# Ranking the first expert's work ahead of the last routing in an attention and mixture-of-experts kernel

## The chip, the cores and the metric

The kernel runs on one core of one Trainium2 chip. The metric is the time of one execution on the device in microseconds (us); a kernel's time is the median of several runs. Beside the runs there is one profiled execution, with a trace of every instruction. The engines are called as in the profile: PE is TensorE (PEld its weight loads), DVE is VectorE, ACT is ScalarE, POOL is GpSimd, and SP is SyncE, which here only issues DMA transfers (SPq in the trace).

## The reference

Two stages. The first is a recurrent attention over 768 steps with a 40 x 40 state per batch entry and head (4 entries, 8 heads):

```python
for t in range(S):
    y[:, :, t] = np.einsum('bhd,bhde->bhe', rt, state)
    Sa = np.einsum('bhde,bhe->bhd', state, at)
    state_decay = state * wt[:, :, None, :] - np.einsum('bhd,bhe->bhde', Sa, bt)
    state = state_decay + np.einsum('bhd,bhe->bhde', vt, kt)
```

Its output is reshaped to 3072 tokens of width 320. The second stage is a mixture of 8 experts. Each token gets noisy logits, `x @ w_gate + log1p(exp(x @ w_noise)) * noise`, and goes to the two experts with the largest ones, with weights from a softmax over the two:

```python
h = np.maximum(x[mask] @ w1[e], 0.0)
out[mask] += top2_w[mask, k, None] * (h @ w2[e])
```

The hidden width is 1024, so w1 is 320 x 1024 and w2 is 1024 x 320 for each expert.

## The kernel before

**Stages.** The attention is computed in chunks of 64 steps. It runs in 24 steps n = 0 to 23 (`Att.run`): 12 chunks for each of two halves of the batch. Each step ends with one tile of 128 tokens (`xt`), which is stored in DRAM (`xd`) and goes to `logits`: three transposes on PE (`px`, L107), a high and a low half of the transposed tile (`xT`; L108 on ACT, L109 on DVE), nine small matmuls (`pl`, L111), and a copy of the 16 logits to `lg` (L115, ACT).

**Routing.** The 24 tiles are routed in groups of 8, 8, 4, 2 and 2 (`RTS`). When a group is complete, `route` finds the top two experts (`gate`: some twenty small DVE instructions and four on ACT), adds the logits to a check sum (`acc`, L133, POOL), counts the tokens for each expert (`cnt`, L135), ranks them with small matmuls against the counts so far (`pr`, L137 to L140), adds the counts to `cumh` (L142, POOL, one addition for each tile of the group), and computes the row `po` at which each entry goes into the experts' list. `scatter` (L162) then writes the entries to that list (`ls`) in DRAM with one indirect DMA on POOL for each tile and choice. The check sum is read only by `flag`, at the end, which decides whether a slower general path must run.

**Two lists.** The list and the token store exist twice. The first 20 tiles (`NA=20`) go to `ls[0]` and `xd[0]`; `turn` then copies the list to `ls[1]`, and the last two groups (tiles 20 and 21, 22 and 23) are scattered only there. The first 512 rows of expert 0 (`PARTS[0]`) are read from `ls[0]` and `xd[0]`, everything else from `ls[1]` and `xd[1]`.

**Experts.** `experts` loads w1 and w2 of an expert (`load1`, L207 and L208; `load2`, L212; on SP). `loadx` loads a part of the expert's index list (`le`, L240, SP) and gathers the tokens, 128 in each indirect DMA on POOL (`xr`, L241). `split1` and `split2` cut the weights into a high part (`w1h`, L218; `w2h`, L226; ACT) and a low part (L219, L220, L227; DVE). `trans` transposes the tokens on PE (`pt`, L254) and splits them (L257 to L261). `hidden` is the first layer: for each of eight blocks of 128 hidden units eight matmuls (`ph`, L273), then the positive part, split into `hh` (L274, ACT) and `hl` (L276, DVE). `output` is the second layer: for each tile of up to 128 tokens 24 matmuls (`po`, L295), a weighting (L296), and an indirect DMA that adds the rows to the output (L297, POOL). An expert has two parts, 512 and 320 rows. For expert 0 the second part is gathered after the last scatter, and its transposes stand after the first part's outputs in the program.

**Memory.** The experts' SBUF and PSUM pools are opened after those of the attention are closed and lie on the same memory. All eight PSUM banks are in use on both sides.

**Order.** The program is traced in Python, and a planner orders each engine's instructions: it simulates the engines, and whenever one is free it issues, of the instructions that its simulation has as ready, the one with the best rank. The rank is the place in the traced program. `high_priority(offset=n)` ranks a block as if it stood n instructions earlier; the chain of the attention's state has 1500 (`PRIO`), and the block of the first expert has `PX`, which is 0. `burst` keeps a group of matmuls together. `issue_after` puts instructions behind a given one on their engine. Each engine then works through its instructions strictly in that order, waiting for semaphores.

Of the kernel before, what the change touches and what calls it, by code (L numbers as in the profile page):

```python
# [13 lines left out]
ALU = mybir.AluOpType  # L14
# [7 lines left out]
NA=20  # L22
FAR=65536
XS,WS=2.0**10,2.0**4
PX=0
SG=1
MRB=1
NOUT=3072+896
# [13 lines left out]
class Moe:  # L42
# [84 lines left out]
    def route(s,n0,T,ps,tag,bufs):  # L127

        nc=s.nc
        w=s.ent[:,n0:n0+T,:,2]  # L130
        lg=s.lg[:,0:T]
        oh=s.gate(lg,s.nz[:,n0:n0+T],T,w[:,:,0],w[:,:,1])
        nc.gpsimd.tensor_tensor(s.acc[:,0:T],s.acc[:,0:T],lg,op=ALU.add)  # L133
        r=lambda name,sh=(8,),dt=F32: s.rp.tile([128,RT,*sh],dt,name=name)[:,0:T]
        cnt=r("cnt",dt=F16); nc.vector.tensor_tensor(cnt,oh[:,:,0],oh[:,:,1],op=ALU.add)  # L135
        pr=ps.tile([128,T,8],F32,name="pr",tag=tag,bufs=bufs)
        nc.tensor.matmul(pr,s.tri,cnt,start=True,stop=False,skip_group_check=True)  # L137
        nc.tensor.matmul(pr,s.ones,s.cumh.rearrange("p (o e)->p o e",o=1).to_broadcast([128,T,8]),start=False,stop=False,skip_group_check=True)
        for j in range(T-1):
            nc.tensor.matmul(pr[:,j+1:],s.ones,cnt[:,j:j+1].to_broadcast([128,T-1-j,8]),start=False,stop=j==T-2,skip_group_check=True)  # L140
        h=s.rp.tile([128,8],F16,name="cumh",bufs=len(RTS)); p=s.cumh
        for j in range(T): nc.gpsimd.tensor_tensor(h,p,cnt[:,j],op=ALU.add); p=h  # L142
        s.cumh=h
        rk=r("rk",(1,8))
        k1,k2=r("k1"),r("k2"); bc=lambda z: z.to_broadcast([128,T,8])
        nc.vector.tensor_tensor(k1,pr,bc(s.lim),op=ALU.is_gt)
        nc.vector.tensor_tensor(k2,pr,bc(s.lim2),op=ALU.is_gt)
        nc.vector.tensor_tensor(k1,k1,bc(s.jump),op=ALU.mult)
        nc.vector.scalar_tensor_tensor(k2,k2,float(FAR),pr,op0=ALU.mult,op1=ALU.add)
        nc.vector.tensor_tensor(rk[:,:,0],k1,k2,op=ALU.add)  # L150
        nc.vector.tensor_tensor(oh,oh,rk.to_broadcast([128,T,2,8]),op=ALU.mult)
        pf=r("pf",(2,)); nc.vector.tensor_reduce(pf,oh,axis=AX.X,op=ALU.add)
        po=s.po[:,n0:n0+T]
        nc.vector.scalar_tensor_tensor(po,pf,float(FAR),s.junk[:,n0:n0+T],op0=ALU.add,op1=ALU.min)
        s.todo+=range(n0,n0+T)
        if n0+T>=(NA if SG else 0):
            with (s.tc.issue_after(s.sg) if s.sg else ExitStack()): s.scatter()
# [165 lines left out]
    def experts(s,after):  # L323
        s.adds={}
        with s.tc.issue_after(after): r1=s.load1(0); r2=s.load2(0)
        with s.tc.high_priority(offset=PX):
            x=s.loadx(0); W1=s.split1(r1); X=s.trans(x[0])
        s.loadx(0,x,1); W2=s.split2(r2)
        for e in range(E_):
            if e+1<E_: r1=s.load1(e+1); xn=s.loadx(e+1); s.loadx(e+1,xn,1); r2=s.load2(e+1)  # L330
            with (s.tc.high_priority(offset=PX) if e==0 else ExitStack()): H0=s.hidden(W1,X,0)
            if e==0: s.output(W2,H0,x,e,0); s.trans(x[0],X,1)
# [549 lines left out]
```

## Time and profile before

| | |
|---|---|
| runs before, us | 1023.14, 1027.94, 1027.19 (median 1027.19) |
| profiled execution, us | 1021.33, its span 1019.5 |
| PE busy | 767.5 us, 75% of the span |
| PE weight load busy | 681.2 us, 67% |
| DVE busy | 492.1 us, 48% |
| ACT busy | 396.1 us, 39% |
| POOL busy | 521.4 us, 51% |
| mean granted PE clock | 0.936 |

The span is from the first to the last instruction of the trace. A row of an engine's order of time reads: start, duration, engine, line, operation, output and input tiles, count, and in brackets how long the engine had been idle before it and what ended that. A row of the waits reads: engine, line, what it waited for, total us, count, longest us. In the chain of waits each row is start, length and what the end of the program was waiting for at that time. The attention's last tile is transposed (L107) at 571.78 us; the last instruction of the trace ends at 1019.5 us.

### The profile page before, as it was taken

The page shows a single profiled execution, that of the slowest core. Times are in us where ns is not written, and L with a number is a line of the kernel's source. Part 1 is how long each engine was busy: PE and PEld are TensorE (multiplying, and loading weights), DVE is VectorE, ACT ScalarE, POOL GpSimd, SP SyncE. Part 2 cuts the span into 40 slices and gives each one's busy share as a digit, 9 for nine tenths or more (in the row PEclk, how much of TensorE's full clock was granted, in tenths as well). Part 3 has the DMA queues.
Part 4 walks back from the last instruction along what each step waited for, and adds up shares of the span by engine and source line. Part 5 has one row for each costly group of instructions (what it writes and reads, how often), then busy time and mean ns, then how long its engine had stood idle before and what let it go on. Part 6 is the DMA issues. An engine that isn't in the chain of part 4 may idle for free.

```text
span 1019.5 us, 25178 instructions
## 1 busy us (share of the span) xinstructions
PE 767.5 (75%) x10506; PEld 681.2 (67%) x10506; DVE 492.1 (48%) x961; ACT 396.1 (39%) x816; POOL 521.4 (51%) x678
## 2 busy tenths in 40 slices
PE   0110117687877687899799379999999999999995
PEld 0110116576666576787688259899999989999995
DVE  9329525355567556447355542643434334443430
ACT  2213213354444344554454322543434334343421
POOL 6259979237967728818874335133333333333313
PEclk9999999797778787999899779999999999999998
DMA  3799963478479557655355843426262525262303
GB/s 96 188 203 226 242 172 90 116 197 225 127 193 241 146 121 204 175 152 146 96 120 148 272 119 68 131 49 150 49 150 49 150 49 149 50 149 51 36 7 40
DMA packets 135264, 136.21 MB, mean 134 GB/s; under 512 B 67392, under 2 KB 114948, under 8 KB 135060
## 3 DMA queue, kind: packets, MB, share of 16 engines
q1 hardware_dynamic: 123492, 117.35, 43.6%
q0 software_dynamic: 11648, 17.15, 9.6%
q8 instruction: 85, 1.39, 0.6%
q14 instruction: 39, 0.32, 0.1%
HBM read 96.48 MB, written 41.37 MB: 135 GB/s over the span
## 4 chain that ended last, share of the span: by engine, by line
PE 43%; POOL 21%; DMA 14%; issue 8%; DVE 6%; SPq 3%; ACT 3%; POOLq 0%; DVEq 0%; ACTq 0%
PE po L295 16%; PE ph L273 12%; POOL Tt L541 7%; POOL X L542 7%; PE pY L441 2%; PE psc L441 2%; PE pW L441 2%; DMA X<-scr 2%; DMA xr<-xd,le 2%; DMA out_dram<-y,le 2%; DMA d_ab<-pk 2%; DMA rawk<-in_fm_dram 2%; PE pt L254 2%; POOL rawk L515 2%; POOL xr L241 1%
## 5 line engine op out<-in xcount | busy, mean ns | idle before, releaser
L297 POOL DMA_INDIRECT out_dram<-y,le x56 | 92.4, 1651 | 201.2 <-ACT y L296 171.9
L276 DVE SCALAR_TENSOR_TENSOR hl<-ph,hh 128x256 fp32r<-128x256 f32 (+1 forms) x128 | 71.0, 556 | 154.0 <-ACT hh L274 153.6
L274 ACT ACTIVATE hh<-ph 128x320 fp32r<-128x320 f32 (+1 forms) x128 | 66.1, 518 | 156.1 <-PE ph L273 155.9
L541 POOL TENSOR_TENSOR Tt<-X 128x30 f32<-128x30 f32 (+9 forms) x180 | 108.8, 604 | 11.8
L542 POOL TENSOR_TENSOR X<-X,Tt 128x30 f32<-128x30 f32 (+9 forms) x180 | 106.3, 590 | 12.6
L241 POOL DMA_INDIRECT xr<-xd,le x56 | 54.0, 965 | 74.4 <-DMA le<-ls 27.9
L441 PEld LDWEIGHTS <-st_ab 120*64 120x64 f16 (+1 forms) x928 | 26.5, 117 | 75.8 <-issue 42.2
L295 PE MATMUL po<-w2h,hh 128*128 128x320 f32 x384 | 74.6, 314 | 0.0
L441 PE MATMUL pQ<-w,dT 128*128 128x40 f16 x1152 | 41.2, 184 | 42.3 <-DMA dT<-scr 33.5
L273 PE MATMUL ph<-xh,w1h 128*128 128x512 f32 (+1 forms) x256 | 71.3, 362 | 0.5 <-ACT xh L257 0.5
L441 PEld LDWEIGHTS <-dT 128*128 128x128 f16 x1152 | 38.2, 100 | 49.6 <-DMA dT<-scr 34.4
L273 PE MATMUL ph<-xh,w1l 128*128 128x512 f32 (+1 forms) x256 | 69.0, 351 | 0.0
L273 PE MATMUL ph<-xl,w1h 128*128 128x512 f32 (+1 forms) x256 | 68.6, 349 | 0.0
L295 PE MATMUL po<-w2l,hh 128*128 128x320 f32 x384 | 68.3, 312 | 0.0
L295 PE MATMUL po<-w2h,hl 128*128 128x320 f32 x384 | 68.1, 309 | 0.0
L441 PE MATMUL psc<-st_ab 120*64 120x64 f16 x384 | 12.6, 215 | 68.1 <-DMA st_ab<-d_ab 29.6
L295 PEld LDWEIGHTS po<-w2h,hh 128*128 128x128 f32 x384 | 61.3, 188 | 3.1
L441 PE MATMUL psc<-RV,uT 128*64 128x128 f32 x384 | 56.5, 294 | 4.1 <-DVE P L665 3.7
L295 PEld LDWEIGHTS po<-w2h,hl 128*128 128x128 f32 x384 | 59.2, 188 | 0.1
L295 PEld LDWEIGHTS po<-w2l,hh 128*128 128x128 f32 x384 | 58.9, 188 | 0.4
L162 POOL DMA_INDIRECT ls<-ent,po x48 | 47.2, 984 | 19.3 <-issue 13.6
L441 PE MATMUL psc<-RV 128*64 128x128 f32 x384 | 56.6, 294 | 0.0
(285 smaller groups left out, 1893.9 us busy)
## 6 DMA issues: line engine op xcount, KB each, us to landing
w2r<-in_w_dram SPq DMA_DIRECT2D x8, 1280.0 KB
RV<-in_rv_dram SPq DMA_DIRECT2D x48, 192.0 KB
rawba<-in_fm_dram SPq DMA_DIRECT2D x24, 360.0 KB
d_ab<-pk SPq DMA_DIRECT2D x24, 360.0 KB
st_ab<-d_ab SPq DMA_DIRECT2D x36, 240.0 KB
w1r<-in_w_dram SPq DMA_DIRECT2D x8, 1024.0 KB
raww<-in_fm_dram SPq DMA_DIRECT2D x12, 365.6 KB
st_ab<-d_ab SPq DMA_DIRECT2D x24, 180.0 KB
```

The source lines that it names most:

```text
L162: st=nc.gpsimd.indirect_dma_start(out=s.ls[s.half],out_offset=OFFS(ap=po[:,j,k:k+1],axis=0),in_=s.ent[:,j,k],in_offset=None)
L241: for k in range(c,c+a): nc.gpsimd.indirect_dma_start(out=x[:p,k],out_offset=None,in_=s.xd[w],in_offset=OFFS(ap=li[:p,k,0:1],axis=0))
L254: for t,p in tiles(t0,n): nc.tensor.transpose(pt[:,t-t0:t-t0+p],x[:p,t//128,f0:f0+128],s.idm[:p,:p])
L273: for i,(a,b) in enumerate(mm): nc.tensor.matmul(ph[:,:n],a,b,start=i==0,stop=i==7)
L274: nc.scalar.activation(hh[:,f,:n],ph[:,:n],AF.Relu)
L276: if c.stop>c.start: nc.vector.scalar_tensor_tensor(o,ph[:,c],0.0,hh[:,f,c].bitcast(F32),op0=ALU.max,op1=ALU.subtract)
L295: nc.tensor.matmul(po[:p],h[:,f,r],w[:,f],start=k==0,stop=k==23); k+=1
L297: st=nc.gpsimd.indirect_dma_start(out=s.out_d,out_offset=OFFS(ap=idx[:p,ii],axis=0),in_=y[:p],in_offset=None,compute_op=ALU.add)
L441: def mm(s,*a,**k): return lambda: s.nc.tensor.matmul(*a,**k)
L515: k1=k_[:,:,:,64*b:64*b+64]; (nc.vector if g in MK else nc.gpsimd).tensor_tensor(k1,k1,G['NH'].rearrange("p (a c b) t->p b c a t",a=3,c=CG ...
L541: eng.tensor_tensor(t,Xt[:,j:j+1,j+1:].to_broadcast([128,j,m]),Xt[:,0:j,j:j+1].to_broadcast([128,j,m]),op=ALU.mult)
L542: s.tl=eng.tensor_tensor(Xt[:,0:j,j+1:],Xt[:,0:j,j+1:],t,op=ALU.add)
```

## The change

Three edits. `PX` goes from 0 to 2500. The check sum of the logits is added on DVE for each of the five groups. The counts are added on DVE for the last group alone (22 + 2 > 22; for the group before it is 20 + 2, which is not), and stay on POOL for the others.

```diff
-PX=0
+PX=2500
@@ route
-        nc.gpsimd.tensor_tensor(s.acc[:,0:T],s.acc[:,0:T],lg,op=ALU.add)
+        nc.vector.tensor_tensor(s.acc[:,0:T],s.acc[:,0:T],lg,op=ALU.add)
@@
-        for j in range(T): nc.gpsimd.tensor_tensor(h,p,cnt[:,j],op=ALU.add); p=h
+        for j in range(T): (nc.vector if n0+T>22 else nc.gpsimd).tensor_tensor(h,p,cnt[:,j],op=ALU.add); p=h
```

`PX` is used in two places of `experts`, which are unchanged. The first covers, for expert 0, the list and the gathers of part 0, the split of w1 and the transposes of part 0. The second covers the first layer of part 0. The loads of w1 and w2, the second part's list and gathers, and the split of w2 are outside both.

```python
with s.tc.issue_after(after): r1=s.load1(0); r2=s.load2(0)
with s.tc.high_priority(offset=PX):
    x=s.loadx(0); W1=s.split1(r1); X=s.trans(x[0])
s.loadx(0,x,1); W2=s.split2(r2)
for e in range(E_):
    ...
    with (s.tc.high_priority(offset=PX) if e==0 else ExitStack()): H0=s.hidden(W1,X,0)
```

## The prediction

> **What bounds the kernel now.** I read the windows around the change from attention to experts first, then each engine's order of time there, then SyncE's waits and the chain of waits. The page gives the span; the windows show where TensorE (PE) is not the bound.
>
> ```profile
> span 1019.5 us, 25178 instructions
> ```
> ```profile
> 576.00:598.00 22.00, 6.89 (x32) 4.58 (x33) 14.09 (x55) 7.88 (x15) 9.47 (x11) 0.50 0.90 287
> 598.00:620.00 22.00, 20.55 (x106) 17.09 (x105) 9.07 (x16) 7.71 (x15) 8.52 (x9) 0.98 0.21 56
> ```
>
> Columns: length, busy us and count of PE, PE weight load, DVE, ACT, POOL, then granted clock, DMA share, GB/s. From 598 on PE is busy 20.55 of 22 us at nearly full clock. Between the attention and the first expert, from 576 to 598, it works 6.89 of 22 us at half clock. Whatever brings the dense part forward is carried to the end, since nothing but PE sets the pace behind it. What filled the gap, PE and then POOL in order of time:
>
> ```profile
> 571.78 0.55 PE L107 MATMUL px<-idm,xt 128*128 128x128 f32 x3 [0.65 <-DVE xt L676]
> 578.25 0.25 PE L111 MATMUL pl<-wg,xT 128*128 128x16 f16 x3 [5.92 <-ACT xT L108]
> 579.79 0.33 PE L111 MATMUL pl<-wg,xT 128*128 128x16 f16 x6 [1.29 <-DVE xT L109]
> 587.70 0.19 PE L137 MATMUL pr<-cnt,tri 128*128 128x16 f16 x1 [7.58 <-DVE cnt L135]
> ...
> 590.26 0.21 PE L317 MATMUL pf<-okh,ones 128*128 128x5 f16 x1
> ...
> 593.02 1.21 PE L254 MATMUL pt<-idm,xr 128*128 128x128 f32 x4 [0.71 <-DMA xr<-xd,le]
> 594.71 2.93 PE L273 MATMUL ph<-xh,w1h 128*128 128x512 f32 x6 [0.47 <-ACT xh L257]
> ...
> 599.78 0.51 PE L273 MATMUL ph<-x,w1h 128*128 128x512 f32 x1 [1.29 <-ACT x L260]
> ```
> ```profile
> 580.42 0.67 POOL L133 TENSOR_TENSOR acc<-acc,lg 128x32 f32<-128x32 f32 x1 [13.73 <-ACT lg L115]
> 582.13 1.48 POOL L241 DMA_INDIRECT xr<-xd,le  x1 [1.03 <-DMA xd<-xt]
> ...
> 586.60 0.95 POOL L241 DMA_INDIRECT xr<-xd,le  x1 [0.30 <-issue]
> ```
>
> The four gathers of expert 0's first 512 rows (L241) need only tokens routed long before, yet they stand behind the check sum (L133), for which POOL sat idle 13.7 us. PE's first expert matmuls wait for those gathers; dense work starts at 599.78. The index list le that the gathers read is not early either, as SyncE's (SP) queue shows:
>
> ```profile
> 567.84 0.38 SPq L207 DMA_DIRECT2D w1r<-in_w_dram  x1
> ...
> 570.51 0.73 SPq L212 DMA_DIRECT2D w2r<-in_w_dram  x1
> 571.29 1.34 SPq L240 DMA_DIRECT2D le<-ls  x1
> ```
> ```profile
> SPq L207 <- PE pgm L442: 4.3, 1, 4.3
> ```
>
> The weight load w1r waited for the last pgm (L442, the reader of the attention's last NG_ tile), because the experts' tiles lie on the attention's memory. The same release holds le and xr, so nothing of the expert moves before 567.84. That caps the gain.
>
> **The change, step by step.** Against the profiled execution: 1021.33 us, span 1019.5 plus 1.83 around it. The median shown, 1027.19, is 5.9 above it; I subtract the same gain from the median.
>
> *Step 1, le on SP.* `loadx(0)` is now ranked 2500 instructions earlier, while the loads of w1r and w2r are outside that block. All three come free at 567.84, so I expect le first, at 567.84 in place of 571.29. The three weight issues slide by le's own issue, at most 1.34 us. A quiet le and the gathers behind it can be read from the chain of waits:
>
> ```profile
> 596.75 1.61 DMA le<-ls
> ...
> 601.71 3.03 DMA xr<-xd,le
> 604.78 0.33 PE pt L254 x2
> ```
> ```profile
> 599.17 0.97 POOL L241 DMA_INDIRECT xr<-xd,le  x1 [4.58 <-DMA le<-ls]
> ```
>
> le landed 1.61 after its issue (596.75 to 598.36), and POOL began 0.81 later. So the first gather may start at 567.84 + 1.61 + 0.81 = 570.3, provided L133 is not in front: it goes to DVE, and POOL has nothing else queued between the scatters before 567 and the last routing's counts and scatters, which the gathers pass. What waits behind a gather that waits for le is only these, and they come ready after 587. On SP le passes the weights alone; the last token store and a fill of the output slide with them and nobody near waits for those.
>
> *Step 2, four gathers on POOL.* Loaded: from the first start, 582.13, to the last transposes fed by them, 593.02, is 10.9. Quiet: three spacings of 1.27 (from 599.17 to 601.71 there are two) plus 3.03 is 6.8. The DMA share of 0.90 over 576 to 598 says loaded: 570.3 + 10.9 = 581.2. The lower end is 577.1.
>
> *Step 3, w1 splits.* In the order of ACT and DVE before:
>
> ```profile
> 575.82 2.00 ACT L218 ACTIVATE w1h<-w1r 128x1024 fp32r<-128x1024 f32 x2 [7.54 <-DMA w1r<-in_w_dram]
> 577.72 0.47 ACT L108 ACTIVATE xT<-px 128x384 f16<-128x384 f32 x1
> 578.29 1.06 ACT L218 ACTIVATE w1h<-w1r 128x1024 fp32r<-128x1024 f32 x1
> 580.15 0.18 ACT L115 ACTIVATE lg<-pl 128x16 f32<-128x16 f32 x1 [0.80 <-PE pl L111]
> 581.15 1.99 ACT L226 ACTIVATE w2h<-w2r 128x640 fp32r<-128x640 f32 x3 [0.81 <-DMA w2r<-in_w_dram]
> ```
> ```profile
> 579.76 1.22 DVE L220 TENSOR_TENSOR w1h<-w1r,w1h 64x1024 fp32r<-64x1024 f32 x1
> ...
> 581.13 0.29 DVE L305 TENSOR_TENSOR fz<-acc 128x128 f32<-128x128 f32 x1
> ...
> 594.69 1.29 DVE L258 TENSOR_TENSOR xl<-pt,xh 128x512 fp32r<-128x512 f32 x2 [3.33 <-ACT xh L257]
> 599.76 1.40 DVE L261 TENSOR_TENSOR x3l<-pt,x 64x512 fp32r<-64x512 f32 x2 [3.78 <-ACT x L260]
> ```
>
> They ended at 580.98 (579.76 + 1.22); with le's 0.4 to 1.34 in front, by 582.3. The gathers come later, so the splits are no bound.
>
> *Step 4, dense start.* From the last transposes (593.02) to dense matmuls (599.78) took 6.8: evictions, six half-clock matmuls, the third transposes. 581.2 + 6.8 = 588.0, or 583.9 with quiet gathers.
>
> *Step 5, the routing that is overtaken.* The third w1h (1.06) now stands ahead of xT, and L220 (1.22) ahead of xT's second half (L109), so pl ends about 0.5 + 1.2 later, at 581.8. From lg (580.15) to pr (587.70) took 7.5; the part-0 evictions add about 2.7 on DVE (the L258 pair 1.29, the L261 pair 1.40). pr becomes ready near 592. PE issues in order: if pr stands before the dense matmuls, they wait until 592.0; if behind, they start at 588.0. I take the middle, 590.0. Behind a waiting pr are queued all of the first layer and the outputs.
>
> *Step 6, what is late next.* The second part of expert 0 needs the last scatter. From pr (587.70) to its transposes (604.78) took 17.1, so it comes at 605 to 609. Cover is the rest of the first layer plus the outputs of part 0:
>
> ```profile
> 606.19 1.83 PE ph L273 x8
> 617.72 1.17 PE ph L273 x8
> ...
> 620.73 11.00 PE po L295 x75
> ```
>
> Eight blocks less the six matmuls done: 58/8 x 1.83 = 13.3; outputs, 4 tiles x 24 x 11.00/75 = 14.1. From 590.0 that lasts until 617.4, so the scatter chain is hidden with 8 us to spare. Without this cover it would show in full.
>
> *Step 7, the additions on DVE.*
>
> ```profile
> L133 POOL TENSOR_TENSOR acc<-acc,lg 128x128 f32<-128x128 f32 (+2 forms) x4 | 1.5, 384 | 2.7 <-ACT lg L115 2.6
> ```
>
> The last check sum cost POOL 0.67; the last two counts are smaller. DVE has no such row; the nearest is L305, 0.29 for a larger tile, so three instructions cost at most 0.9, beside 14.1 of 22 us busy, and only if all sit on the routing's path. The four earlier check sums free 1.5 us of POOL and 2.7 of its waiting, and cost DVE at most 1.2. Bounds: 4.2 faster, 2.1 slower. I take 0, since none of these instructions feeds the attention, and DVE has room beside them (14.1 of 22).
>
> **Sum:** 599.8 - 590.0 = 9.8 us. 1021.33 - 9.8 = 1011.5 profiled; median 1027.2 - 9.8 = 1017.4.
>
> *A rule against it.* The page's windows give the clock 0.50 while PE idles, and the six matmuls took 2.93 us, where eight take 1.83 in the dense part. The Trainium skill ("TensorE: Matmul & The Clock Gate", "Part 1: The HAM clock gate") says that an idle window of about 3.4 us halves the clock and as long a busy one restores it; the trace agrees. By that rule a first layer held up by pr starts cold again and loses some 1.7 us (an estimate from that page), a gain of 8.1 instead of 9.8. Since the first six matmuls were cold before too, I leave that out.
>
> **Rivals.**
>
> *A, slower: pl falls behind the whole first layer.* Line 331's block is ranked ahead of the last logits as well; if PE's order puts all 64 matmuls before pl, they run 588.0 to 601.3. Then pl to pf took 12.0 (578.25 to 590.26), and the outputs lie on the PSUM of the logits and flags: they begin near 614.2 and end at 628.3. Part 1 comes at 601.3 + 26.5 (578.25 to 604.78) = 627.8, and its transposes and evictions end about 631.2. Before, the same point is 620.73 + 11.00 less two blocks of the second part already done (1.17 each): 629.4. So 1.8 slower, 1029.0. It decides from pl later than 599.5. For it: priority. Against: xT is ready near 580, while the first layer still lacks gathers; PE is free then.
>
> *B: only pr falls behind the first layer.* pr at 601.3, part 1 at 618.4, outputs from about 604.8 to 618.9, second part from 621.8: 7.6 faster, 1019.6. For it: pr and the dense start come ready within 4 us of each other.
>
> *C: the change doesn't do what it says: le stays behind the weights.* Its gathers then start when le lands. If that is quick, 571.29 + 1.61 + 0.81 = 573.7 puts the dense start at 591.4, still inside the forecast. But the start at 582.13, a full 1.03 after L133 ended, fits a le that landed only then; so late, nothing is won. For it: SP issued them in that order before. Against: the rank. With a late le it is 0 to 1 faster, 1027.
> The Trainium skill ("DMA: Bandwidth & Descriptors", "Queues, rings and completion order") says that one issuer's descriptors are consumed in ring order. By it le behind w2r lands no sooner than that load, whose reader started at 581.15; no row of le's landing settles that.
>
> **How the numbers follow.** Forecast 55%, quiet gathers 3% (15.9 faster, 1011.3), A 10%, B 20%, C 12%. About 0.5% (5.1 us) is what a measurement of this kernel tells from no change. Faster: the forecast and the quiet case nearly whole, most of B, 0.74. Same: C, most of A and some of B, 0.19. Slower: A together with the slower end of step 7, 0.07. The likeliest case alone spans 584 to 592 at the dense start, 7.8 to 15.9 faster: 1011 to 1019. With the runs' own spread (1023.1 to 1027.9) and most of C, the range is 1010 to 1026.
>
> **What would show it.** Step 1: le ahead of w1r on SP at about 568. Step 2: POOL's first L241 near 570, no L133 on POOL. Step 4: dense PE from 588 to 592, expert stages unchanged behind it. Step 5: where pl and pr stand among the first layer's matmuls. Step 6: no PE idle before part 1's transposes. I am wrong if le is not first, if pl comes after 599.5, or if the attention itself ends elsewhere than 571.8.

## The result and the profile after

The changed kernel took 1019.1 us (median of 19 runs, 1015.57 to 1025.81), the kernel before 1025.36 us beside it (19 runs, 1021.36 to 1039.52). The ratio is 0.995, 95% interval 0.9932 to 0.9968: by it 5.1 us faster, 3.3 to 7.0; the two medians differ by 6.3. Ratios here and below leave out runs that took over 1.5% more than the fastest of their kernel (one run of e9_w2_again took 3869.47 us). The prediction was 1017.4 us and 9.8 faster.

The profiled execution of the changed kernel took 1022.5 us. Its attention ended later than that of the profiled execution before (px at 575.07, not 571.78) at a lower granted clock (0.929 over the whole, not 0.936). So the two traces are compared from a point that both have: the **release**, when SyncE issues the first transfer into the memory that the attention gives back. It was 567.84 before (w1r) and is 569.64 after (le).

SyncE's order of time, changed kernel; then POOL's and ACT's:

```profile
565.89 0.46 SPq L101 DMA_DIRECT2D out_dram<-dm  x1
569.64 0.32 SPq L240 DMA_DIRECT2D le<-ls  x1
570.01 0.52 SPq L207 DMA_DIRECT2D w1r<-in_w_dram  x1
...
572.93 0.59 SPq L212 DMA_DIRECT2D w2r<-in_w_dram  x1
```
```profile
576.77 1.00 POOL L241 DMA_INDIRECT xr<-xd,le  x1 [7.24 <-PE px L107]
```
```profile
580.03 3.12 ACT L218 ACTIVATE w1h<-w1r 128x1024 fp32r<-128x1024 f32 x3 [9.95 <-DMA w1r<-in_w_dram]
...
586.53 1.36 ACT L226 ACTIVATE w2h<-w2r 128x640 fp32r<-128x640 f32 x2 [3.00 <-DMA w2r<-in_w_dram]
...
587.87 1.35 ACT L226 ACTIVATE w2h<-w2r 128x640 fp32r<-128x640 f32 x2
589.12 1.07 ACT L257 ACTIVATE xh<-pt 128x512 fp32r<-128x512 f32 x2
```

The index list le is issued first, as forecast, but the first gather starts 7.1 us behind it (569.64 to 576.77). The page names px as what released POOL; px had begun 1.7 us earlier, and the gather needs nothing of it: in the run e1_rank_only below it starts before px (574.98 and 576.58). What it lacked was le, as the experiments show. On ACT the four pieces of the second weight's split (w2h) stand ahead of xh, the first eviction of the gathered rows.

TensorE's order of time, changed kernel:

```profile
585.55 1.52 PE L254 MATMUL pt<-idm,xr 128*128 128x128 f32 x6
589.75 2.93 PE L273 MATMUL ph<-xh,w1h 128*128 128x512 f32 x6 [2.68 <-ACT xh L257]
...
594.82 0.79 PE L273 MATMUL ph<-x,w1h 128*128 128x512 f32 x1 [1.29 <-ACT x L260]
...
600.99 0.18 PE L137 MATMUL pr<-cnt,tri 128*128 128x16 f16 x1
...
602.24 0.73 PE L273 MATMUL ph<-xh,w1h 128*128 128x512 f32 x2 [0.96 <-DVE hl L276]
...
625.66 1.15 PE L254 MATMUL pt<-idm,xr 128*128 128x128 f32 x6
```

The transposes end at 587.07 (585.55 + 1.52), xh starts 2.05 later. Dense matmuls start at 594.82, that is 25.2 us behind the release; before it was 31.9 (567.84 to 599.78). So 6.8 us are won there. But the rest of the program grew. From the dense start to the end of the span it took 419.7 us before (599.78 to 1019.5) and takes 425.9 now (594.82 to 1020.7). Two windows, first before and then after, show one cause (columns as in the prediction):

```profile
599.78:605.05 5.27, 5.11 (x25) 4.00 (x25) 2.02 (x4) 1.28 (x3) 2.24 (x3) 1.00 0.30 78
```
```profile
594.82:599.00 4.18, 4.18 (x10) 3.31 (x11) 2.21 (x9) 0.18 (x1) 0.00 (x0) 0.50 0.89 269
599.00:604.00 5.00, 4.04 (x23) 3.11 (x22) 2.74 (x15) 1.57 (x3) 0.00 (x0) 0.99 0.02 7
```

Before, the dense part began at full clock: the granted clock had risen at 598.74, 1.0 us ahead of it, and the first ten matmuls took 2.42 us (599.78 to 602.20). Now the clock rises only at 599.07, 4.3 us behind the dense start, and the same ten take 4.35 us (594.82 to 599.17).

### The profile page after: what moved, and what is told of

Same layout as the page of the kernel before. It is cut to its first block, busy times and chain, and to the rows that moved or that the text cites. A ratio compares the mean times of both kernels' runs of the same rounds, so it can differ in the third digit from the quotient of the medians.

```text
span 1020.7 us, 25175 instructions
## 1 busy us (share of the span) xinstructions
PE 775.9 (76%) x10506; PEld 688.1 (67%) x10506; DVE 493.1 (48%) x968; ACT 396.5 (39%) x816; POOL 519.7 (51%) x671
## 4 chain that ended last, share of the span: by engine, by line
PE 42%; POOL 25%; issue 12%; DMA 12%; DVE 5%; SPq 2%; ACT 1%; POOLq 0%; DVEq 0%; ACTq 0%
PE po L295 15%; PE ph L273 13%; POOL X L542 8%; POOL Tt L541 8%; DMA rawk<-in_fm_dram 3%; PE psc L441 2%; PE pY L441 2%; DMA xr<-xd,le 2%; DMA X<-scr 2%; POOL xr L241 2%; PE pW L441 2%; DMA rawba<-in_fm_dram 2%; PE pt L254 2%; POOL rawk L515 1%; POOL rawba L489 1%
## 5 line engine op out<-in xcount | busy, mean ns | idle before, releaser
L542 POOL TENSOR_TENSOR X<-X,Tt 128x30 f32<-128x30 f32 (+9 forms) x180 | 110.9, 616 | 12.6
L541 POOL TENSOR_TENSOR Tt<-X 128x30 f32<-128x30 f32 (+9 forms) x180 | 104.5, 580 | 12.0
L441 PE MATMUL psc<-RV,uT 128*64 128x128 f32 x384 | 59.5, 304 | 4.4 <-DVE P L665 4.1
L441 PE MATMUL psc<-RV 128*64 128x128 f32 x384 | 59.5, 304 | 0.0
```

The source lines that it names most:

```text
L441: def mm(s,*a,**k): return lambda: s.nc.tensor.matmul(*a,**k)
L541: eng.tensor_tensor(t,Xt[:,j:j+1,j+1:].to_broadcast([128,j,m]),Xt[:,0:j,j:j+1].to_broadcast([128,j,m]),op=ALU.mult)
L542: s.tl=eng.tensor_tensor(Xt[:,0:j,j+1:],Xt[:,0:j,j+1:],t,op=ALU.add)
```

## The experiments

All times in the table come from the profiled execution of each run, in us behind that run's own release; the last two columns are the stretch from the dense start to the end of the span, and the timed ratio to the kernel before with its interval. The runs were spread over several chips, and each ratio is to the kernel before on the same chip. The three marked * were on one where the kernel before took 1075.9 us.

| run | release | first gather | w1 split | xh | dense start | dense start to end | ratio |
|---|---|---|---|---|---|---|---|
| before | 567.84 | 14.3 | 8.0 | 26.2 | 31.9 | 419.7 | 1 |
| changed | 569.64 | 7.1 | 10.4 | 19.5 | 25.2 | 425.9 | 0.995 (0.9932 to 0.9968) |
| e1_rank_only | 572.37 | 2.6 | 6.0 | 15.2 | 20.9 | 423.8 | 0.9933 (0.9899 to 0.9967) |
| e2_adds_only | 569.93 | 13.0 | 6.6 | 25.0 | 30.8 | 421.9 | 1.0006 (0.9976 to 1.0036) |
| e3_w2_behind | 564.87 | 4.4 | 8.1 | 15.1 | 20.8 | 427.1 | 0.990 (0.9861 to 0.994) |
| e4_fill_early | 570.66 | 3.7 | 5.9 | 15.4 | 21.3 | 422.8 | 0.9952 (0.9918 to 0.9986) |
| e5_le_apart * | 617.82 | 0.7 | 7.3 | 17.9 | 23.6 | 426.2 | 0.9938 (0.9908 to 0.9969) |
| e6_both * | 617.02 | 0.7 | 6.4 | 14.9 | 20.6 | 425.5 | 0.9925 (0.9895 to 0.9955) |
| e7_warm * | 625.17 | 4.8 | 7.0 | 16.5 | 22.2 | 424.0 | 0.9908 (0.9875 to 0.994) |
| e8_after_again | 568.52 | 6.3 | 10.3 | 19.2 | 25.0 | 424.9 | 0.9949 (0.9915 to 0.9983) |
| e9_w2_again | 566.32 | 4.6 | 7.7 | 14.7 | 20.4 | 423.3 | 0.9954 (0.9925 to 0.9984) |
| e10_rank_w2 | 573.50 | 4.6 | 7.6 | 14.3 | 20.0 | 424.9 | 0.9936 (0.9906 to 0.9966) |
| e11_w2_load_late | 568.26 | 0.7 | 9.7 | 14.7 | 20.6 | 427.7 | 0.9896 (0.9852 to 0.994) |
| e12_fill_one | 568.84 | 3.7 | 6.6 | 14.0 | 19.4 | 424.2 | 0.9899 (0.9847 to 0.995) |

The theory at the outset (T1): the rank brings the gain, the additions nothing. Rivals: freeing POOL of the check sum brings it (T2); the additions change the planner's order in the attention, and that costs or gives some 2 us (T3).

### The rank alone, and the additions alone

e1_rank_only is the changed kernel without its additions:

```diff
-        nc.vector.tensor_tensor(s.acc[:,0:T],s.acc[:,0:T],lg,op=ALU.add)
+        nc.gpsimd.tensor_tensor(s.acc[:,0:T],s.acc[:,0:T],lg,op=ALU.add)
...
-        for j in range(T): (nc.vector if n0+T>22 else nc.gpsimd).tensor_tensor(h,p,cnt[:,j],op=ALU.add); p=h
+        for j in range(T): nc.gpsimd.tensor_tensor(h,p,cnt[:,j],op=ALU.add); p=h
```

> The rank alone: PX is 2500, and the check sums (L133) and last counts (L142) stay on POOL. Theory T1 (the rank brings the gain, the additions nothing): a ratio to the kernel before of 0.993 to 0.997, as the changed kernel's 0.995; le is issued first at the release of the pool, the first gather starts within 6 us of the last px (L107), and expert 0's first-layer matmuls start 18 to 21 us after that px, where before it was 22.9 for the six small ones (571.78 to 594.71). Rival T2 (taking L133 off POOL brings it): 0.998 to 1.002, with the gathers behind L133 still near px + 10. Rival T3 (the additions on DVE change the order inside the attention and cost some 2 us there): the rank alone is 1 to 2 us better than the changed kernel, ratio 0.992 to 0.994, with the last px earlier than in the changed kernel (575.07) at an equal clock.

e2_adds_only is the changed kernel without its rank:

```diff
-PX=2500
+PX=0
```

> The additions alone: L133 and the last counts on DVE, PX stays 0. T1: no change, 0.999 to 1.001, since the gathers stay behind the routing in rank. T2 (POOL is free of L133, so the gathers go as soon as le is there): the first gather no longer waits for the last lg, 3 to 5 us faster, ratio 0.995 to 0.997. T3 (a changed order in the attention costs 1 to 2 us): 1.001 to 1.002, with the last px 1 to 2 us later than 571.78 at an equal clock.

The rank alone gave 0.9933, the additions alone 1.0006. POOL's order with the rank alone:

```profile
574.98 1.00 POOL L241 DMA_INDIRECT xr<-xd,le  x1 [6.08 <-PE psc L441]
...
583.52 0.24 POOL L133 TENSOR_TENSOR acc<-acc,lg 128x32 f32<-128x32 f32 x1 [3.78 <-ACT lg L115]
```

The gathers overtake the sum of the logits (L133) though it is still on POOL. With the additions alone, POOL is free of it, and still the first gather comes late. SyncE's, ACT's and POOL's order of e2_adds_only:

```profile
574.33 0.58 SPq L240 DMA_DIRECT2D le<-ls  x1
```
```profile
581.94 2.62 ACT L226 ACTIVATE w2h<-w2r 128x640 fp32r<-128x640 f32 x4 [1.15 <-DMA w2r<-in_w_dram]
```
```profile
582.91 1.49 POOL L241 DMA_INDIRECT xr<-xd,le  x1 [15.06 <-ACT w2h L226]
```

Here le is issued behind w2r. The reader of w2r starts at 581.94, the gather 1.0 later and 8.6 us after le's issue. The trace also records each single DMA packet. Here le's 128 packets of 64 bytes run from 580.60 to 581.59, where the packets of w2r come to their end; in the kernel before they run from 579.29 to 580.84, issued at 571.29. So the check sum, which the prediction named as what the gathers stand behind, was not what held them before; le was. T1 holds and T2 falls. T3 can't be told apart at this width: 1.0006 allows 2.5 us faster to 3.7 slower, and the position of the last pY moves with the clock. In the traces the rank alone did better than the changed kernel (dense start 20.9 us behind the release, where the two profiles of the changed one have 25.2 and 25.0), because le and w1r landed sooner; the timed ratios do not tell the two apart.

### The second weight's split behind the rows

```diff
-                for q in (slice(0,64),slice(64,128)): nc.scalar.activation(x3[q,r],pt[64:128,:n],AF.Copy)
+                for q in (slice(0,64),slice(64,128)): s.x3i=nc.scalar.activation(x3[q,r],pt[64:128,:n],AF.Copy)
...
-        s.loadx(0,x,1); W2=s.split2(r2)
+        with ExitStack() as c: s.loadx(0,x,1); c.enter_context(s.tc.issue_after(s.x3i.ins)); W2=s.split2(r2)
```

> The changed kernel with the ACT part of the second weight's split (w2h, L226) queued behind the last copy of x (L260) in place of ahead of the first eviction of the gathered rows (xh, L257). Theory (xh stands ready behind two w2h on ACT: transposes end near 586.6, xh runs at 589.1): xh comes 2 to 2.5 us earlier against the last px, the six small matmuls too, and the kernel is 2 to 3 us faster than the changed one, ratio 0.992 to 0.994. Rival (the routing of the last tokens, pr, or the outputs' need of w2h sets the pace next): xh is earlier but the outputs are not, ratio 0.995 as before. Second rival (w2h now comes too late for the outputs, which wait for it): 0.996 or above, with PE idle ahead of the first po.

The ratio was 0.990. It was run again beside the changed kernel, and with the additions back on POOL:

> The changed kernel once more, unaltered, beside the next three on one chip, so that they can be compared with it directly. If the first comparison holds: ratio to the kernel before 0.993 to 0.997, first-layer matmuls (the six small ones) 16 to 17 us and dense matmuls 21 to 22 us behind the last pY (L441).

> e3_w2_behind once more, unaltered. If the second weight's split on ACT is what held xh: 2 to 6 us below e8_after_again on the same chip, dense matmuls 15 to 16 us behind the last pY. Rival (its earlier 0.990 was the spread of a few runs): within 2 us of e8_after_again.

> The kernel before with the rank and with the second weight's split behind the last copy of x; the additions stay on POOL. Theory (the additions give and cost nothing): the same as e9_w2_again within 2 us. Rival T3 (the additions' changed order in the attention costs 1 to 2 us): 1 to 2 us below e9_w2_again, with the last pY earlier at an equal clock. Rival T2 (L133 on POOL holds the gathers of the second part or the scatters): 1 to 3 us above it.

TensorE's and ACT's order of e9_w2_again:

```profile
579.55 1.52 PE L254 MATMUL pt<-idm,xr 128*128 128x128 f32 x6
...
586.73 0.79 PE L273 MATMUL ph<-x,w1h 128*128 128x512 f32 x1 [1.18 <-ACT x L260]
```
```profile
581.03 1.07 ACT L257 ACTIVATE xh<-pt 128x512 fp32r<-128x512 f32 x2
```

The transposes end at 581.07 and xh is there: the 2.05 us of the changed kernel are gone, and from the last transposes to dense matmuls it takes 7.2 (579.55 to 586.73) in place of 9.3 (585.55 to 594.82). That the split held xh is shown. What it is worth in time is not: the first run gave 0.990, the second 0.9954 beside 0.9949 for the changed kernel on the same chip. The rival of the expectation (the spread of a few runs) holds for the time. e10_rank_w2 (0.9936) and e9_w2_again agree within their intervals, and so do their dense starts (20.0 and 20.4), so the additions again show no effect.

### The index list, the weights and the fill of the output

Three runs ask why le is late. One moves all four fills of the output (L101, 1280 KB each) eight steps earlier, one gives le memory of its own, so that it is loaded long before, one joins this with the split behind the rows:

```diff
-ZN=20
+ZN=12
```

> The changed kernel with its four fills of the output (L101) eight steps earlier in the attention (ZN 12 in place of 20), so that none of them is under way when le and w1r are issued. Theory (le took 6.4 us from its issue at 569.64 to landing because a 1280 KB fill was still in the queues): le lands in 2 to 3 us, the first gather starts near px + 0 in place of px + 1.7 at the latest, w1r lands 2 to 3 us earlier and so do w1h and the transposes; 2 to 4 us faster than the changed kernel where nothing else holds xh, 0.991 to 0.994. Rival (le is late behind the loads issued with it, or xh is held by the w2 split on ACT in any case): no change, 0.994 to 0.996. Second rival: the fills in the middle of the attention cost there, 0.996 to 0.998.

```diff
-            NTT=-(-s.cap//128); l=s.xp.tile([128,NTT,4],F32,name="le",bufs=2); x=s.xp.tile([128,NTT,DM],F32,name="xr")
+            NTT=-(-s.cap//128); l=s.kp.tile([128,NTT,4],F32,name="le0") if e==0 and s.cap==CAP else s.xp.tile([128,NTT,4],F32,name="le",bufs=2); x=s.xp.tile([128,NTT,DM],F32,name="xr")
```

> The changed kernel with expert 0's index list le in memory of its own (112 bytes a partition beside the constants) in place of the pool that the attention holds: it is loaded ahead of the list's snapshot (L125), long before the release. Theory (the first gather waits for le's landing, 7.1 us from its issue at 569.64 to 576.77): the first gather starts within 1.5 us of the first weight load's issue, the first transposes some 7.2 us behind it as in the four runs with the rank, xh at the end of the w1h split, and dense matmuls 3 to 5 us earlier against the last pY (L441); ratio to the kernel before 0.990 to 0.993. Rival (the split of the first weight, whose load landed only at 580, or the second weight's split on ACT holds xh in any case): the gathers move, xh does not; 0.994 to 0.996. Second rival (gathers and weights share the transfer engines, so the weights land later by what the gathers gain): the w1h split starts later against the weight's issue, no change.

> le apart (as in e5_le_apart) and the second weight's split behind the last copy of x (as in e3_w2_behind) together, on the changed kernel. Theory (two separate delays of one path): dense matmuls 1 to 3 us earlier against the last pY than with the second alone (10.3 us there), ratio 0.987 to 0.990. Rival (with w2h out of the way the first weight's landing bounds xh, and le no longer counts): as e3_w2_behind, 0.990. Second rival (dense work ahead of the routing gives its gain back in the clock and in later gaps): the dense start moves, the stage behind it grows by as much, 0.990 or above.

SyncE's, POOL's and TensorE's order of e5_le_apart:

```profile
617.82 0.38 SPq L207 DMA_DIRECT2D w1r<-in_w_dram  x1
```
```profile
618.56 1.00 POOL L241 DMA_INDIRECT xr<-xd,le  x1 [2.48 <-ACT xt L674]
```
```profile
627.40 0.66 PE L254 MATMUL pt<-idm,xr 128*128 128x128 f32 x2 [2.25 <-DMA xr<-xd,le]
```

With le there in time, the first gather starts 0.74 us behind the release (also in e6_both and e11_w2_load_late). So xr's memory is free at once, and the 2.6 to 7.1 us of the other ranked runs are le's landing. But the rows took longer to come: the first transposes start 8.8 us behind the first gather (618.56 to 627.40), where the changed kernel took 7.1 (576.77 to 583.88), and the last packet of the rows runs 10.6 us behind it in e5_le_apart and e6_both (629.20 and 628.34), 8.8 in the changed kernel (585.53). So the dense start of e5_le_apart came 1.4 to 1.6 us earlier, not the 3 to 5 expected, and e6_both's (20.6) is no better than that of e3_w2_behind (20.8). The rival of its expectation holds in that le no longer counts; but what held xh in e6_both was not the weight. TensorE's order there:

```profile
630.27 0.33 PE L111 MATMUL pl<-wg,xT 128*128 128x16 f16 x6 [0.88 <-DVE xT L109]
630.44 1.09 PE L254 MATMUL pt<-idm,xr 128*128 128x128 f32 x4
```

The last four transposes stood behind the last logits (pl), which waited for xT.

That w2r's load takes the engines from w1r and the rows was tried by issuing it later:

```diff
-        with s.tc.issue_after(after): r1=s.load1(0); r2=s.load2(0)
+        with ExitStack() as c: c.enter_context(s.tc.issue_after(after)); r1=s.load1(0); c.enter_context(s.tc.issue_after(s.xw.ins)); r2=s.load2(0)
```

> e6_both with the second weight's load (w2r, 1280 KB) issued behind the attention's last token store in place of right behind the first weight's. Theory (w2r shares the transfer engines with the first weight and the gathers, some 3.4 MB in all, and w2r is 1.3 of it): the first weight's split starts 2 to 3 us after the load's issue sooner than the 6.4 us it took there (617.02 to 623.40), the transposes likewise, and dense matmuls come 1 to 3 us earlier than pY + 15.2; ratio 0.985 to 0.990. Rival (the last px and the routing's matmuls stand between the transposes and are not ready sooner): the loads land sooner, the dense start does not move, as e9_w2_again. Second rival (w2h comes too late, or the routing falls behind the first layer, and the outputs or the second part's transposes wait): PE idle ahead of po or behind it, ratio 0.992 or above.

```profile
577.97 2.00 ACT L218 ACTIVATE w1h<-w1r 128x1024 fp32r<-128x1024 f32 x2 [9.27 <-DMA w1r<-in_w_dram]
```

The row is from ACT's order. w1r was issued at 568.26 and its reader starts 9.7 us later, not sooner but 3.3 later than in e6_both (6.4). The theory fell. The slow cases have a fill closer ahead: it was issued 3.8 us before w1r here (564.50), 4.1 in the changed kernel (565.89 to 570.01; 10.0 to the reader), 5.4 in e6_both. The fill's own packets explain little of it, though: its last one starts at 569.67 here, w1r's first 0.1 later and 1.5 behind w1r's issue, where it is 1.1 in e6_both. The rest is in w1r's packets, which run for 10.9 us here (569.78 to 580.66), 9.6 in the changed kernel, 8.0 in e6_both and 5.4 in e1_rank_only. What stretched them was not found.

The list was set against the **fill's** issue in the same way. These are the seven ranked runs with le in the pool and a fill within 8 us ahead; the last two columns are from the records of single packets, in us behind le's issue:

| run | fill issued | le issued | first gather | behind le | behind the fill | last packet of the fill | le's packets, first to last |
|---|---|---|---|---|---|---|---|
| changed | 565.89 | 569.64 | 576.77 | 7.1 | 10.9 | +1.4 | 1.5 to 5.6 |
| e8_after_again | 564.77 | 568.52 | 574.84 | 6.3 | 10.1 | +1.4 | 1.5 to 4.9 |
| e3_w2_behind | 559.88 | 564.87 | 569.27 | 4.4 | 9.4 | +0.1 | 1.0 to 3.0 |
| e10_rank_w2 | 568.73 | 573.50 | 578.10 | 4.6 | 9.4 | +0.4 | 1.0 to 3.2 |
| e7_warm | 620.16 | 625.17 | 629.99 | 4.8 | 9.8 | +0.1 | 1.0 to 3.4 |
| e9_w2_again | 560.74 | 566.32 | 570.94 | 4.6 | 10.2 | -0.5 | 0.9 to 2.6 |
| e1_rank_only | 565.27 | 572.37 | 574.98 | 2.6 | 9.7 | -2.0 | 0.9 to 1.2 |

Whenever le goes out, its gather starts 9.4 to 10.9 us behind the fill's issue. That looks as if le always waited for the fill; the packets say otherwise. Only in the two profiles of the changed kernel is the fill still under way when le could begin: its last packet starts at 571.07 and le's first at 571.13 (569.94 and 570.03 in the second), so that le begins 1.5 us behind its issue in place of 0.9. That costs some 0.6 us. In the other five le begins 0.9 to 1.0 behind its issue, as it does without a fill near. What differs is when its last packets run. In the changed kernel 120 of the 128 had started by 571.84, the last eight from 575.15 on. Two windows of it, first the fill, then the wait for those eight (the second line there is SyncE's queue: packets, MB, share of the 16 engines):

```profile
DMA packets 2144, 1.32 MB, mean 320 GB/s; under 512 B 93, under 2 KB 2144, under 8 KB 2144
```
```profile
DMA packets 82, 0.33 MB, mean 107 GB/s; under 512 B 1, under 2 KB 1, under 8 KB 82
q1 hardware_dynamic: 81, 0.33, 89.1%
```

They are 567.00 to 571.12 and 571.90 to 575.00. In the second the 16 transfer engines are busy for 89.1% of the time with 81 packets of w1r, and move a third of the bytes a second. In every run the gather starts 1.3 to 2.0 us behind le's last packet, so these last packets set it.

The last run moves that one fill alone, on top of e9_w2_again:

```diff
-                if ZN<=n<ZN+4:
-                    with after(m.xw.ins): m.zero(n-ZN)
+                if n in ZN:
+                    with after(m.xw.ins): m.zero(ZN.index(n))
...
-ZN=20
+ZN=19,20,21,23
```

> e9_w2_again with one of the four fills of the output (L101, 1280 KB) moved: the one behind the last but one tile's store, which goes out 4 to 6 us ahead of le, goes out three tiles earlier; the others stay. Theory (le and the first weight stand in SyncE's queue behind that fill: in the seven runs with it the first gather starts 9.4 to 10.9 us after the fill's issue and the first weight's split 11.8 to 14.1, whatever le's and the weight's own issue): the first gather starts 2.4 to 3.7 us after le's issue (4.4 and 4.6 in the two runs with the fill), the first weight's split 5.5 to 6 us after the weight's first issue (7.7 and 7.3), and dense matmuls come 1.5 to 2.5 us earlier than pY + 15.4 and 16.2; 1 to 2 us below the kernels without it, ratio to the kernel before 0.988 to 0.994. Rival (le and the weight are slow because the transfers issued after them share the engines): landings and dense start as before, 0.990 to 0.995.

Its SyncE, POOL, ACT and TensorE, in order of time:

```profile
554.36 0.42 SPq L101 DMA_DIRECT2D out_dram<-dm  x1
568.84 0.32 SPq L240 DMA_DIRECT2D le<-ls  x1
569.22 1.52 SPq L207 DMA_DIRECT2D w1r<-in_w_dram  x1
```
```profile
572.49 1.00 POOL L241 DMA_INDIRECT xr<-xd,le  x1 [5.72 <-issue]
```
```profile
575.39 2.00 ACT L218 ACTIVATE w1h<-w1r 128x1024 fp32r<-128x1024 f32 x2 [6.10 <-DMA w1r<-in_w_dram]
```
```profile
588.26 0.50 PE L273 MATMUL ph<-x,w1h 128*128 128x512 f32 x1 [1.18 <-ACT x L260]
```

The gather starts 3.7 us behind le, w1r's reader 6.2 behind its issue (7.3 in e9_w2_again, so the 5.5 to 6 of the expectation is missed by a little), and the dense start is 19.4 us behind the release, the earliest of all. But le's first packet starts 0.9 behind its issue here as in e9_w2_again, and its last 1.9 where it was 2.6; so this run does not show a wait for the fill, and the 1.0 us of the dense start is no more than the ranked runs differ by. Without a fill near, le still took 3.7 to the gather (also in e4_fill_early), against the 2.4 that the prediction used, and e1_rank_only, with a fill, took 2.6. The Trainium skill ("DMA: Bandwidth & Descriptors", "Queues, rings and completion order") says that on each transfer engine the descriptors of one issuer are consumed in ring order; the changed kernel agrees, where le's first packet follows the fill's last by 0.06 us.

What spreads le's packets stays open. One thing goes with it: in eight of the nine ranked runs with le in the pool, a packet of 16 KB of the queue that the page calls instruction starts between le's issue and its last packet (at 571.37 in the changed kernel) and takes 0.9 to 2.2 us; in e1_rank_only none does, and all 128 packets start within 0.24 us. The weight behind le is not needed for it: in e9_w2_again le's packets spread over 1.7 us, and w1r's start only after them. No run varied the instruction packets alone.

e4_fill_early moved all four fills and gained nothing more: dense start at 21.3, ratio 0.9952. There xt was planned behind the first weight's splits on DVE, so that px came 5.9 us behind the last pY (1.8 in the changed kernel), and the transfers ran in the middle of the attention. What each of the two cost was not separated.

### A warm clock

```diff
-            for t,p in tiles(t0,n): nc.tensor.transpose(
+            for t,p in list(tiles(t0,n))*(3 if k==1 and s.adds=={} else 1): nc.tensor.transpose(
```

> The changed kernel with the four transposes of the gathered rows' second third done three times over, so that TensorE is busy for some 2 us more just ahead of the first-layer matmuls, while it waits for xh behind the second weight's split. Nothing is left out; eight transposes are added, at 0.25 us each. Theory (the clock stands at 0.50 until 599 because TensorE idled for 2 us before ph and for 2.3 before the dense start): the granted clock rises some 3 to 5 us earlier, the six small matmuls take 1.6 in place of 2.93 us, the dense start comes 1 to 1.5 us earlier and its first blocks run at 0.61 us a pair in place of 1.05; 2 to 3 us faster than the changed kernel, ratio 0.992 to 0.994. Rival (the clock does not answer to so little work, or the pause before the dense start lowers it again): no change, 0.994 to 0.997.

Windows of e7_warm (the six small matmuls, the third transposes, the first dense matmuls), and the first dense matmuls of e9_w2_again:

```profile
642.29:645.01 2.72, 2.72 (x6) 2.04 (x7) 2.72 (x11) 0.97 (x4) 0.00 (x0) 0.50 1.06 418
645.01:647.36 2.35, 1.06 (x6) 0.66 (x4) 1.59 (x15) 1.22 (x3) 0.00 (x0) 0.79 1.03 257
647.36:650.00 2.64, 2.64 (x11) 2.17 (x12) 2.21 (x9) 0.17 (x1) 0.00 (x0) 1.00 1.06 357
```
```profile
586.73:590.00 3.27, 3.27 (x8) 2.59 (x9) 3.23 (x8) 2.59 (x4) 0.00 (x0) 0.50 0.68 183
```

The dense part of e7_warm starts at full clock, but the six matmuls ahead of it were still at half (0.50), where they were expected at full. That the added work did this is not shown, since e4_fill_early, e6_both and e12_fill_one start at full clock without it. The ratio, 0.9908, does not stand out from the others' intervals.

What the clock costs can be read from e9_w2_again and e12_fill_one, which have the same work on TensorE. Their first ten dense matmuls take 4.43 us (586.73 to 591.16) and 2.38 (588.26 to 590.64): 2.0 us. The windows from the dense start to the end, in that order:

```profile
586.73:1010.00 423.27, 407.06 (x2455) 375.64 (x2455) 168.31 (x323) 163.79 (x297) 147.43 (x112) 0.98 0.37 86
```
```profile
588.26:1012.50 424.24, 405.66 (x2455) 373.96 (x2455) 168.28 (x323) 163.59 (x297) 147.19 (x112) 0.99 0.37 86
```

Over the whole stretch the same 2455 rows keep TensorE busy for 407.06 us from a cold start and for 405.66 from a warm one, 1.4 us; other small differences of the two runs are in that.

## Why the prediction was right or wrong

**Direction and cause** were right: faster, within the range, by the rank and not by the additions. What had held the gathers was not the check sum, which the prediction put first, but le behind w2r, which it weighed under rival C and left open. That the forecast median, 1017.4, lies 1.7 us from the measured 1019.1 is partly luck: the gain was 5.1 us by the ratio and not 9.8, and the kernel before took 1025.36 beside it in place of 1027.19.

**Step 1 (le on SP)** had the order right and the landing wrong: 7.1 us to the first gather (6.3 in the second profile), not 1.61 + 0.81. The row of a quiet le was taken. Of the 4.7 us more, the fill's packets ahead of le account for some 0.6; SyncE had issued one at 563.06, 4.8 ahead of the release, and it was not in the sum. Most of the rest is le's last eight packets, 3.3 us behind the others, whose cause is open. Rival C weighed the ring order, but only for le behind w2r.

**Step 2 (four gathers)**: 8.8 us from the first gather to the last transposes (576.77 to 585.55), not 10.9; it lies between the quiet 6.8 and the loaded value.

**Step 3 (w1 splits)**: ACT's part ended at 583.15, not by 582.3: w1r's packets ran from 571.24 to 580.80. It set nothing, as forecast.

**Step 4 (dense start)**: 9.3, not 6.8. The evictions now stood behind the second weight's split. Its row (w2h at 581.15) was quoted in the prediction, as work that was over before the rows came; with the rows earlier it was in front of them.

**Step 5 (the overtaken routing)**: the dense matmuls did not wait for pr, so the 2.0 us added for it were not spent. pr ran at 600.99, behind three of eight blocks: rival B's order in part, without its price.

**Step 6 (what's late next)** held. Part 1's rows were gathered from 613.32 on, later than 605 to 609, and the outputs covered them: TensorE reached their transposes at 625.66 without a wait.

**Step 7 (additions)** at 0 agrees with e2_adds_only.

Steps 1 to 5 together put the dense start 22.2 us behind the release (590.0 less 567.84); it was 25.2 and 25.0. So 3 us are missing there, of errors that partly cancel: 4.7 too little in step 1 and 2.5 in step 4, against 2.1 too much in step 2 and 2.0 in step 5. (In rival A the outputs would by its own terms begin at 601.3 + 12.0 = 613.3, not 614.2; that changes nothing, since part 1 sets its end.)

**The step that failed most was one that the sum did not have**: that the part behind the dense start stays as it was. It grew by 6.2 us (419.7 to 425.9) and by 5.2 in the second profile (424.9). The window from the dense start to the end, before and after, and a row of TensorE's order in the latter:

```profile
599.78:1019.50 419.72, 403.95 (x2454) 373.91 (x2454) 164.55 (x311) 161.21 (x293) 141.35 (x108) 0.99 0.36 82
```
```profile
594.82:1020.70 425.88, 407.69 (x2460) 375.62 (x2460) 167.35 (x338) 161.18 (x294) 146.10 (x112) 0.98 0.37 83
```

```profile
629.45 0.41 PE L273 MATMUL ph<-x,w1h 128*128 128x320 f32 x1 [0.97 <-ACT x L260]
```

TensorE's busy time there went from 403.95 to 407.69 us. Of these 3.7, some 1.9 are the half clock (the first ten matmuls took 4.35 in place of 2.42), and at most 0.5 the six matmuls of the routing that now lie behind the dense start (2460 rows in place of 2454; five of them overlap and end 0.29 us after pr starts, the sixth took 0.18). The other 1.3 are not placed. Its idle time went from 15.8 to 18.2 us: 1.0 is new ahead of the fourth block, whose PSUM buffer waits for hl (the row at 602.24), and 1.0 ahead of part 1's x (the row at 629.45). The prediction had the half clock as a rule against the change, at 1.7, and left it out because the six small matmuls had been cold before too; but the 58 behind them had been warm. The size was nearly right, and the omission wrong. Its condition (a first layer held up by pr) was not met either; the clock was still at half because the dense part began before it rose, and in the kernel before it had risen only 1.0 us ahead.

**What stays open.** From the release to the end of the span it took 451.7 us before and 452.7 in e2_adds_only, 451.1 and 449.9 in the two profiles of the changed kernel: about 1.7 us less, where the timed runs give 5.1. Each profile is one execution, and the runs of one kernel lie 10 us apart (1015.57 to 1025.81; the first at a mean granted clock of 0.938, the profiled one, 1022.5, at 0.929). The remaining 3.4 us were not found. Nor do the timed ratios of the ranked kernels, 0.9896 to 0.9954, tell them apart: their intervals overlap, though the dense start moved by 5.8 us among them. The best median beside its own kernel before is e12_fill_one's, 1014.8 to 1027.14.

## What to carry to other kernels

When work is moved ahead, follow its inputs to the queue that brings them and look there at when their own packets ran, the last ones above all: a small list counted as quiet was late here though it was issued first, and a large transfer ahead of it explained only a part. Then see what else was hidden in the wait that goes away: work that came ready in the gap (here the second weight's split) now stands in front. And price the part behind the moved work anew, since a gap in TensorE's work that ends in a different place changes the clock with which the next part starts.

## What was unexpected of the hardware

**A small transfer is as late as its last few packets.** The same list of 128 packets of 64 bytes took 2.6 to 7.1 us from issue to use in the nine ranked runs where it is issued at the release. Its first packet started 0.9 to 1.5 us behind the issue in all of them, its last 1.2 to 5.6.

**When the clock comes up differs by 6 us with the same work.** In all fourteen traces the changes of the granted clock lie whole multiples of 3.41 us apart. Windows between such points, first of e12_fill_one, then of e9_w2_again:

```profile
583.10:586.51 3.41, 2.99 (x8) 2.31 (x9) 3.23 (x21) 1.06 (x3) 0.00 (x0) 0.50 1.16 344
586.51:588.26 1.75, 0.57 (x9) 0.47 (x7) 1.10 (x13) 1.21 (x3) 0.00 (x0) 1.00 1.04 417
```
```profile
581.07:584.48 3.41, 2.81 (x7) 2.13 (x8) 3.25 (x21) 1.24 (x4) 0.00 (x0) 0.50 1.15 353
587.89:591.30 3.41, 3.41 (x10) 2.63 (x9) 3.38 (x8) 1.43 (x3) 1.08 (x1) 0.50 0.27 65
591.30:592.30 1.00, 1.00 (x6) 0.83 (x5) 0.11 (x1) 0.00 (x0) 0.99 (x1) 1.00 0.00 0
```

In e12_fill_one the clock was up 3.0 us after the first of the six small matmuls (583.52 to 586.51). In e9_w2_again, with the same instructions in the same order on TensorE from the end of the attention on, it came up 9.6 us after it (581.66 to 591.30). The Trainium skill ("TensorE: Matmul & The Clock Gate", "Part 1: The HAM clock gate") says that the window by which activity is judged runs freely, so that the moment depends on where in it the work begins; the two runs fit that. How busy a window must be was not measured, and the pause ahead of the first transposes differed too (2.2 and 5.3 us).

**Engines can stop for nothing that the trace shows.** On the other chip TensorE and DVE stood for long stretches of the attention while POOL issued its 32 scatters. TensorE's and DVE's order and a window of e5_le_apart:

```profile
532.49 0.66 PE L441 MATMUL pQ<-w,dT 128*128 128x40 f16 x15 [16.99 <-issue]
```
```profile
532.47 0.49 DVE L599 SCALAR_TENSOR_TENSOR w<-pW,w 128x320 f16<-128x320 f32 x1 [25.95 <-issue]
```
```profile
512.00:532.00 20.00, 2.08 (x7) 0.89 (x8) 0.00 (x0) 0.00 (x1) 15.12 (x17) 0.50 0.03 2
```

For 20 us TensorE worked 2.08 and DVE not at all, with the transfer engines at 3%. All three profiles from that chip show the low busy time there (60.5 to 62.4 us of TensorE from 450 to 550, where the changed kernel on the first chip has 92.4). The cause was not looked for.
